# A decay-attention, mixture-of-experts and bilinear kernel: first weights kept unsplit in DRAM, and a new order of the main stage

## The chip, the cores and the metric

The kernel runs on one core of one Trainium2 chip. The metric is device time in microseconds (us) of one execution, from repeated runs; a profile of one more execution shows where that time lies. The engines are TensorE (PE, matrix products; PEld are its weight loads), VectorE (DVE), ScalarE (ACT), GpSimd (POOL) and SyncE (SP, which here only issues transfers).

## The reference

Three parts follow each other, all in 32-bit floats:

```python
# 1. attention with decay: B, H, S, D = 4, 8, 768, 48
f = 1.0 / (1.0 + np.exp(-f_logit))
for t in range(S):
    state = f[:, :, t, :, None] * state + np.einsum('bhd,bhe->bhde', k[:, :, t], v[:, :, t])
    y[:, :, t] = np.einsum('bhd,bhde->bhe', q[:, :, t], state)
x = y.transpose(0, 2, 1, 3).reshape(3072, 384)
# 2. eight experts, weights P from 8 rounds of normalising rows and columns
P = sinkhorn(x @ w_gate)
out = sum(P[:, e:e + 1] * (np.maximum(x @ w1[e], 0.0) @ w2[e]) for e in range(8))   # w1[e]: 384 x 1024
# 3. bilinear
return (out @ w_a) * (out @ w_b) @ w_out                                            # w_a, w_b: 384 x 1536
```

## The kernel before

Every product is made from numbers split in two: a high half `wh`, `xh` rounded to TensorE's fast 32-bit format and a low half `wl`, `xl` that holds the rest. A product costs three matmuls (high by high, high by low, low by high), and ScalarE makes the high half by a copy, VectorE or GpSimd the low half by a subtraction.

An attention stage comes first (to about 421 us); beside it TensorE works on most of expert 0. Everything else is the **main stage**, which this change is about. It has six phases: three of the experts (`moe`, 1024 tokens each) and three of the bilinear part (`out`). A phase is a row of jobs, 19 for `moe`, 8 for `out`, 81 in all. A job has a front and a back.

- `front(n)` (line 975) multiplies a 384 x 384 block of the first weights with the phase's tokens by a fast scheme: 15 products in place of 18 (`CHAINS`), each of three matmuls with 512 columns (`mm`, line 998). For it the block's nine 128 x 128 pieces are turned into 15 sums (`W_SUMS`: 13 additions or subtractions in a buffer `stage` of 15 x 128 columns), and the tokens into 15 sums `xs`. Results stand in banks of PSUM named `pG` and `pF`; ScalarE and VectorE take them into a ring of 19 buffers `z`, handed out by `take_z`/`free_z`.
- `back` (line 1055) splits those results (`halve`: ScalarE, then VectorE or GpSimd) and multiplies them with the second weights in matmuls of 384 columns into `pR` (`gemm_t`, line 368); VectorE adds each `pR` into `acc`.

The first weights of a job are the same in the three phases of its kind. In the first of them (27 jobs: `first_of[kind, u] == n`) `w1_load` (line 814) fetches the pieces into `stage`, `w1_split` (line 844) makes the sums and then, for three groups of 768, 512 and 640 columns (`W_GROUPS`), the halves in `w1t[n % 2]`; `w1_store` (line 865) writes both halves, 1920 KB, to a DRAM buffer `wfd` after chain 9 of the front. In the other 54 jobs `w1_load` fetches both halves back in three transfers and nothing is split. Loads and splits of job n + 2 are put into the list beside the front of job n.

At a phase's start `x_take` (line 902) fetches the 15 sums of the tokens through temporary buffers and splits them; in phases 1, 2, 4 and 5 three of these are cut out of `stage`, which then has no other use. `x_make` (line 879, GpSimd) makes those sums ahead of time, `convert` (line 958) turns 64-bit weights of the bilinear part into 32 bits by seven VectorE steps (lines 311 to 319) during the expert phases, `x2` (line 1117) transposes a phase's result.

The order of every engine's instructions is a list written before the run. `plan.add` records each step with a priority, an engine, a cost and what it reads and writes; `Plan.order` (line 131) plays the steps through and, whenever an engine is free, takes the ready step of least priority. It counts a step as ready some time after its sources end, and a transfer as landed 5 us after it is issued, whatever its size:

```python
    plan = Plan(.4, 1.5, port=True, stay=STAY)   # .4 us from engine to engine, 1.5 us to SP
    LATE = 5.0
...
                far = self.hold if self.ops[u][1] == "SP" else self.slack if ever else self.gap
                gap = late + (far if self.ops[u][1] != eng else 0.0 if eng == "PE" else self.same)
                ready_at[u] = max(ready_at[u], at + cost + gap)
```

Costs marked `"DVE+"` and all of GpSimd's are kept from overlapping in this list. All instructions of line 1203 are those that the main stage's list issues.

## Time and profile before

| | us |
|---|---|
| median of 3 runs (2183.95 to 2189.29) | 2189.18 |
| the profiled execution | 2187.57 |
| its span, first to last instruction | 2185.8 |
| PE busy in the span | 2159.0 |
| DVE, ACT, POOL busy | 1610.4, 942.2, 910.4 |
| moved by transfers | 413.43 MB |

A busy PE is not a PE at its peak, since its matmuls overlap in a pipeline; how fast it goes is read from how long a run of matmuls takes. Idle time of another engine costs nothing by itself.

### The profile page before, as it was taken

The page shows a single profiled execution, that of the slowest core. Times are in us where ns is not written, and L with a number is a line of the kernel's source. Part 1 is how long each engine was busy: PE and PEld are TensorE (multiplying, and loading weights), DVE is VectorE, ACT ScalarE, POOL GpSimd, SP SyncE. Part 2 cuts the span into 40 slices and gives each one's busy share as a digit, 9 for nine tenths or more (in the row PEclk, how much of TensorE's full clock was granted, in tenths as well). Part 3 has the DMA queues.
Part 4 walks back from the last instruction along what each step waited for, and adds up shares of the span by engine and source line. Part 5 has one row for each costly group of instructions (what it writes and reads, how often), then busy time and mean ns, then how long its engine had stood idle before and what let it go on. Part 6 is the DMA issues. An engine that isn't in the chain of part 4 may idle for free.

```text
span 2185.8 us, 41932 instructions
## 1 busy us (share of the span) xinstructions
PE 2159.0 (99%) x15933; PEld 1961.6 (90%) x15933; DVE 1610.4 (74%) x2888; ACT 942.2 (43%) x1779; POOL 910.4 (42%) x924
## 2 busy tenths in 40 slices
PE   8999999999999999999999999999999999999999
PEld 8999999989999999898999988999999888888888
DVE  7878888387878778676787697677776866866755
ACT  3544454454444445433334344433343545533331
POOL 2212121378876664431222255433222577634322
PEclk9999999999999999999999999999999999999999
DMA  6556653456765558875454466666443555787552
GB/s 138 112 118 147 174 122 80 140 201 214 253 245 188 208 187 302 288 250 186 141 173 157 158 225 235 219 218 215 165 163 127 185 203 193 283 284 255 173 173 73
DMA packets 318346, 413.43 MB, mean 189 GB/s; under 512 B 146880, under 2 KB 207936, under 8 KB 314688
## 3 DMA queue, kind: packets, MB, share of 16 engines
q1 hardware_dynamic: 302832, 393.97, 56.0%
q10 hardware_dynamic: 15312, 16.78, 2.2%
q8 instruction: 125, 2.05, 0.4%
q14 instruction: 77, 0.63, 0.1%
HBM read 279.33 MB, written 126.62 MB: 186 GB/s over the span
## 4 chain that ended last, share of the span: by engine, by line
PE 93%; DVE 3%; DMA 2%; SPq 1%; ACT 0%; issue 0%; POOL 0%; ACTq 0%; DVEq 0%
PE pR L368 39%; PE pG L998 27%; PE pF L998 10%; PE pM L356 4%; PE pM L368 3%; PE pT L482 1%; PE pA L525 1%; PE pO L638 1%; PE pA L537 1%; PE pO L610 1%; PE pA L569 1%; PE pO L644 1%; PE pA L580 1%; DVE z L1203 1%; PE pO L682 1%; PE pM L729 0%
## 5 line engine op out<-in xcount | busy, mean ns | idle before, releaser
L368 PE MATMUL pR<-er 128*128 128x384 f32 x5052 | 976.2, 336 | 2.9 <-DVE acc L1203 2.7
L368 PEld LDWEIGHTS pR<-er 128*128 128x128 f32 x5052 | 897.9, 188 | 55.2 <-DVE acc L1203 3.0
L1203 POOL TENSOR_TENSOR er<-z,er 128x512 fp32r<-128x512 f32 x221 | 299.3, 1367 | 659.6 <-ACT er L1203 512.8
L1203 ACT ACTIVATE z<-pG 128x512 f32<-128x512 f32 x474 | 282.8, 599 | 658.6 <-PE pG L998 578.2
L1203 DVE SCALAR_TENSOR_TENSOR acc<-pR,prob,acc 128x384 f32<-128x384 f32 x504 | 305.2, 612 | 194.4 <-PE pR L368 192.8
L998 PE MATMUL pG<-xsh,w 128*128 128x512 f32 x1134 | 431.4, 394 | 5.9 <-ACT z L1203 5.8
L1203 ACT ACTIVATE er<-z 128x512 fp32r<-128x512 f32 x420 | 248.8, 625 | 143.4 <-PE pR L368 107.9
L1203 DVE TENSOR_TENSOR z<-pF,z 128x512 f32<-128x512 f32 x324 | 221.3, 687 | 93.6 <-PE pF L998 70.3
L998 PE MATMUL pG<-er,w 128*128 128x512 f32 x972 | 278.8, 395 | 1.2 <-DVE z L1203 0.8
L998 PEld LDWEIGHTS pG<-xsh,w 128*128 128x128 f32 x1134 | 212.7, 188 | 42.1 <-ACT z L1203 8.1
L1203 DVE TENSOR_TENSOR z<-z,pG 128x512 f32<-128x512 f32 x243 | 166.2, 685 | 84.7 <-PE pG L998 81.2
L998 PE MATMUL pG<-xsl,w 128*128 128x512 f32 x567 | 223.8, 395 | 0.0
L998 PEld LDWEIGHTS pG<-er,w 128*128 128x128 f32 x972 | 180.0, 188 | 32.8 <-DVE z L1203 3.7
L708 POOL TENSOR_TENSOR er<-l,er 128x256 fp32r<-128x256 f32 x84 | 71.7, 854 | 281.0 <-ACT l L706 249.5
L1203 DVE SCALAR_TENSOR_TENSOR er<-z,er 128x512 fp32r<-128x512 f32 x171 | 171.6, 1014 | 6.2 <-ACT er L1203 5.2
L1203 POOL TENSOR_TENSOR stage<-stage 128x128 f32<-128x128 f32 x325 | 158.9, 521 | 38.9 <-DMA stage<-in_moe_w_dram 28.9
L1203 DVE TENSOR_TENSOR z<-pG,z 128x512 f32<-128x512 f32 x174 | 119.9, 689 | 67.3 <-PE pG L998 64.5
L1203 POOL TENSOR_TENSOR w<-stage,w 128x768 fp32r<-128x768 f32 (+2 forms) x75 | 124.1, 1662 | 43.4 <-ACT w L1203 38.8
L998 PE MATMUL pF<-er,w 128*128 128x512 f32 x486 | 139.0, 394 | 1.4 <-DVE z L1203 1.4
L326 POOL TENSOR_TENSOR er<-raw,er 128x384 fp32r<-128x384 f32 (+1 forms) x82 | 94.5, 1157 | 98.5 <-ACT er L324 84.6
L998 PE MATMUL pF<-xsh,w 128*128 128x512 f32 x324 | 126.9, 393 | 0.0
L998 PEld LDWEIGHTS pG<-xsl,w 128*128 128x128 f32 x567 | 106.3, 188 | 10.7
(166 smaller groups left out, 2594.2 us busy)
## 6 DMA issues: line engine op xcount, KB each, us to landing
er<-w2d SPq DMA_DIRECT2D x138, 384.0 KB, 4.5
wfmoe<-w SPq DMA_DIRECT2D x19, 1920.0 KB, 7.8
w<-wfmoe SPq DMA_DIRECT2D x38, 768.0 KB, 5.2
w2d<-er SPq DMA_DIRECT2D x69, 384.0 KB, 4.0
w<-wfmoe SPq DMA_DIRECT2D x38, 640.0 KB, 4.9
w<-wfmoe SPq DMA_DIRECT2D x38, 512.0 KB, 4.3
wfout<-w SPq DMA_DIRECT2D x8, 1920.0 KB, 7.5
raw<-in_moe_w_dram SPq DMA_DIRECT2D x64, 192.0 KB, 2.9
```

The source lines that it names most:

```text
L326: plan.add(prio + 1, "POOL", S_COST[0] + m * S_COST[1], [gk, key], [key], lambda: nc.gpsimd.tensor_tensor(out=lj, in0=got, in1=f32(hj), op ...
L356: nc.tensor.matmul(out=ps, lhsT=a[:, kk, fs], rhs=b[:, kk, :], start=(i == 0), stop=(i == 3 * KD - 1),)
L368: nc.tensor.matmul(out=ps, lhsT=a[:, off:off + 128], rhs=b, start=(start and i == 0), stop=(stop and i == n - 1))
L482: nc.tensor.transpose(ps[0:R, p * 128:p * 128 + 128], src[:, p * 128:p * 128 + R], ident)
L525: nc.tensor.matmul(out=A0[o:o + 64, w, :], lhsT=pct(bk)[r, g, :], rhs=pct(bq)[r, g, :])
L537: nc.tensor.matmul(out=A1[o:o + 56, 0, w, :].rearrange("j (b e) -> j b e", e=8), lhsT=pct(k3)[r, g, 0:56], rhs=qv[r, g, :, 1, :])
L569: nc.tensor.matmul(out=A1[o:o + 48, 1, w, :].rearrange("j (b e) -> j b e", e=16), lhsT=pct(k3)[r, g, 0:48], rhs=qv[r, g, :, 1, :])
L580: nc.tensor.matmul(out=A1[o:o + 32, 0, w, :], lhsT=pct(k3)[r, g, 0:32], rhs=pct(q3)[r, g, 32:64])
L610: nc.tensor.matmul(out=ps[64 * hd:64 * hd + m, p * D:(p + 1) * D], lhsT=kn[64 * c:64 * c + 64, p * R + 64 * hd:p * R + 64 * hd + m], rhs=b ...
L708: op(POOL, .76, [f"hh{ft}", kf], [f"hl{ft}"], lambda hh=hh, hl=hl, hf=hf: nc.gpsimd.tensor_tensor(out=hl, in0=hf, in1=f32(hh), op=ALU.subt ...
L998: nc.tensor.matmul(out=ps, lhsT=a[:, slot], rhs=b, start=(new and i == 0), stop=(i == 2), skip_group_check=not new)
L1203: fn()
```

## The change

Three things, all of the main stage but for the jobs 0 and 1, whose weights are loaded and split in the attention stage.

- **Sums kept unsplit.** `wfd` holds the 15 sums as they stand in `stage` (960 KB a job). They are stored straight after the sums are made; `w1_store` is gone. The other 54 jobs load the three groups into `stage` (384, 256 and 320 KB) and split them as the first jobs do: three copies on ScalarE and three subtractions on GpSimd a job.
- **Temporary buffers.** `stage` is now in use in all phases, so `x_take` has three buffers of the ring `z` in its place at each of the five later phases, taken before the phase's first front.
- **The list.** The main stage is ordered by a new function, `Plan.timed(.03, .3)`. It has tables of how long steps take: `TAKES` by engine and planned cost, and for TensorE `COLUMNS` per matmul with a few ns more at the start of a run (`AFTER`). To another engine go `WAY` and .03 us in place of .4; to SP .3 in place of 1.5. Transfers stand in one queue of 330 GB/s, with 1.93 us of way and .001 us a piece, by sizes from `moves`. VectorE's `"DVE+"` steps and GpSimd's still exclude each other. Priorities and the rule that prefers to stay with one kind of matmul for `STAY` = 1.2 us are the same.

```diff
@@ -97,7 +97,7 @@
     SWITCH = .02
 
     def __init__(self, gap=GAP, hold=GAP, same=SAME, over=0.0, ranked=False, early=0, slack=None, port=False, stay=0.0):
-        self.port, self.shared, self.stay, self.kind = port, set(), stay, {}
+        self.port, self.shared, self.stay, self.kind, self.key = port, set(), stay, {}, {}
         self.ranked, self.early, self.slack = ranked, early, slack or gap
         self.gap, self.hold, self.same, self.over = gap, hold, same, over
         self.ops = []
@@ -106,6 +106,7 @@
     def add(self, prio, eng, cost, reads, writes, fn, late=0.0, fill=False, kind=0):
         n = len(self.ops)
         self.kind[n] = kind
+        self.key[n] = next(iter(writes), ""), len(writes)
         if self.port and eng in ("POOL", "DVE+"):
             self.shared.add(n)
         eng = eng.rstrip("+")
@@ -199,6 +200,106 @@
                     todo.setdefault(self.ops[u][1], []).append(u)
         return made
 
+    ENGINES = ("PE", "DVE", "ACT", "POOL", "SP", "clock")
+    WAY = {"PE": .205, "DVE": .115, "ACT": .125, "POOL": .085}
+    RUNS = {.681: (512, 3), 1.362: (512, 6), .522: (384, 3), 1.044: (384, 6), .53: (384, 3), 1.06: (384, 6),
+            .36: (256, 3), .72: (256, 6), 1.08: (256, 9)}
+    COLUMNS = {512: .2267, 384: .1733, 256: .12}
+    AFTER = {512: (3.7, 6.7, 6.7, -1.2, 4.2, 8.7, 2.5, 5.0, 3.3, 0.0), 384: (-2.5, 3.7, 6.2, 2.5, 3.7, .8, 0.0),
+             256: (2.0,), "pause": (6.0, 6.2, 3.3, 7.5, 3.3, 2.5, 2.5, 2.0, 0.0)}
+    TAKES = {
+        "PE": {.2: .117, .33: .245, .35: .2, .69: .713},
+        "DVE": {.62: .528, .56: .467, .68: .602, .69: .603, .7: .603, .93: .91, 1.0: 1.016, .204: .22, .255: .28, .3: .24, .383: .3},
+        "ACT": {.6: .52, .45: .387, .49: .387, .521: .414, .612: .53, .737: .635, .863: .735, .37: .263, .47: .395, .25: .27},
+        "POOL": {.46: .417, 1.026: .977, 1.252: 1.256, 1.29: 1.256, 1.54: 1.522, 1.828: 1.81, .76: .72},
+        "SP": {.36: .46, .38: .47, .4: .42, .42: .4, .41: .43, .43: .42, .45: .615, 1.2: 1.23, 2.4: 2.5},
+    }
+    DMA_WAY, DMA_RATE, DMA_PIECE = 1.93, 330e3, .001
+
+    def moves(self, n):
+
+        _, eng, cost, _, _, late, _ = self.ops[n]
+        (key, many), cost, kb = self.key[n], round(cost, 3), 1024
+        if eng == "ACT":
+            return (256 * kb, 128) if key[:2] == "xd" else (128 * kb, 128)
+        if cost == .45:
+            return (1920 * kb, 128) if key[:2] == "wf" else (128 * kb * {"0": 6, "1": 4, "2": 5}[key[-1]], 256)
+        if cost == .41:
+            return 64 * kb * many, 128
+        if cost == .43:
+            return 960 * kb, 128
+        if cost == .38:
+            return 384 * kb, 128
+        if key[:2] == "pb":
+            return 256 * kb, 512
+        return (256 * kb if cost == .4 and key[:2] != "sg" else 192 * kb), 128
+
+    def timed(self, near, far, shift={}):
+
+        left, users, ready = [], [[] for _ in self.ops], [0.0] * len(self.ops)
+        todo = {eng: [] for eng in self.ENGINES}
+        prio = [o[0] + shift.get(n, 0) for n, o in enumerate(self.ops)]
+        for n, o in enumerate(self.ops):
+            left.append(len(o[3]))
+            for d in o[3]:
+                users[d].append(n)
+            if not o[3]:
+                todo[o[1]].append(n)
+        free, port, queue, run, now, made = dict.fromkeys(self.ENGINES, 0.0), 0.0, 0.0, 0.0, 0, []
+        width, place, paused = 0, 0, False
+        while any(todo.values()):
+            best = None
+            for eng, ns in todo.items():
+                if ns:
+                    soon = min(ready[n] for n in ns)
+                    at = soon if eng == "clock" else max(free[eng], soon)
+                    if best is None or at < best[0]:
+                        best = (at, eng)
+            at, eng = best
+            n = min((n for n in todo[eng] if ready[n] <= at + 1e-9),
+                    key=lambda n: (eng == "PE" and (self.kind[n] == now) != (run < self.stay), prio[n]))
+            todo[eng].remove(n)
+            cost, late = round(self.ops[n][2], 3), self.ops[n][5]
+            if n in self.shared:
+                at = max(at, port - .03)
+            if eng == "PE" and cost in self.RUNS:
+                cols, count = self.RUNS[cost]
+                if width != cols:
+                    width, place, paused = cols, 0, False
+                if at > free["PE"] + .04:
+                    place, paused = 0, True
+                more = self.AFTER["pause" if paused else cols]
+                takes = 0.0
+                for _ in range(count):
+                    takes += self.COLUMNS[cols] + .001 * more[min(place, len(more) - 1)]
+                    place += 1
+            else:
+                takes = self.TAKES.get(eng, {}).get(cost, cost)
+                if eng == "ACT" and late and cost == .45:
+                    takes = .42
+                if eng == "PE":
+                    width, place, paused = 0, 0, False
+            if n in self.shared:
+                port = max(port, at + takes)
+            if self.kind[n]:
+                run = takes + (run if self.kind[n] == now else 0.0)
+                now = self.kind[n]
+            free[eng] = end = at + takes
+            made.append(self.ops[n][4])
+            dma = eng == "SP" or (eng == "ACT" and late > 0)
+            if dma:
+                size, pieces = self.moves(n)
+                queue = max(end + self.DMA_WAY - .03, queue) + size / self.DMA_RATE + pieces * self.DMA_PIECE
+                end = queue + .03
+            for u in users[n]:
+                to = self.ops[u][1]
+                way = 0.0 if dma or (eng == to and eng != "SP") else self.WAY.get(eng, 0.0) + near
+                ready[u] = max(ready[u], end + way + (far if dma or to == "SP" else 0.0))
+                left[u] -= 1
+                if not left[u]:
+                    todo[to].append(u)
+        return made
+
 
 @with_exitstack
 def tile_decay_attention__then__sinkhorn_moe__then__bilinear_kernel(
@@ -806,7 +907,7 @@
             for u in range(DFF2 // 384):
                 for n in range(2):
                     jobs.append((ph, 2 * u + n, [(n, 384 * u + 128 * f) for f in range(3)], n))
-    wfd = {k: [spill.tile([128, 2, NW, 128], F32, name=f"wf{k}{u}") for u in range(n)] for k, n in (("moe", len(moe_blocks) // 3), ("out", 2 * DFF2 // 384))}
+    wfd = {k: [spill.tile([128, NW, 128], F32, name=f"wf{k}{u}") for u in range(n)] for k, n in (("moe", len(moe_blocks) // 3), ("out", 2 * DFF2 // 384))}
     first_of = {}
     for n, (ph, u, _, _) in enumerate(jobs):
         first_of.setdefault((phases[ph][0], u), n)
@@ -818,8 +919,8 @@
         wh, wl = w1s[n % 2]
         if first_of[kind, u] != n:
             for g, (lo, hi) in enumerate(W_GROUPS):
-                plan.add(prio + W_STEP * g, SP, .45, [f"wf{kind}{u}"], [f"w1{n % 2}{g}"], partial(
-                    nc.sync.dma_start, out=f32(w1t[n % 2][:, :, lo:hi]), in_=wfd[kind][u][:, :, lo:hi]), LATE)
+                plan.add(prio + W_STEP * g, SP, .41, [f"wf{kind}{u}"], [f"sg{x}" for x in range(lo, hi)], partial(
+                    nc.sync.dma_start, out=stage[:, lo:hi], in_=wfd[kind][u][:, lo:hi]), LATE)
             return
         runs = []
         for f, (e, c) in enumerate(blocks):
@@ -845,14 +946,15 @@
 
         ph, u, _, _ = jobs[n]
         kind = phases[ph][0]
-        if first_of[kind, u] != n:
-            return
         wh, wl = w1s[n % 2]
         tt, cs, cl = (nc.gpsimd.tensor_tensor, .46, .00225) if eng == POOL else (nc.vector.tensor_tensor, .26, .0012)
 
-        for i, (o, a, how, b) in enumerate(W_SUMS):
+        for i, (o, a, how, b) in enumerate(W_SUMS if first_of[kind, u] == n else ()):
             plan.add(prio + i, eng, cs, [f"sg{a}", f"sg{b}"], [f"sg{o}"], partial(
                 tt, out=stage[:, o], in0=stage[:, a], in1=stage[:, b], op=getattr(ALU, how)))
+        if first_of[kind, u] == n:
+            plan.add(prio + 15, SP, .43, [f"sg{x}" for x in range(NW)], [f"wf{kind}{u}"], partial(
+                nc.sync.dma_start, out=wfd[kind][u], in_=stage), LATE)
         for g, (lo, hi) in enumerate(W_GROUPS):
             m, at = (hi - lo) * 128, prio + 20 + W_STEP * g
             sg = [f"sg{x}" for x in range(lo, hi)]
@@ -861,14 +963,6 @@
             plan.add(at + 1, eng, .1 + m * cl, sg, [f"w1{n % 2}{g}"], partial(
                 tt, out=wl[:, lo:hi], in0=stage[:, lo:hi], in1=f32(wh[:, lo:hi]),
                 op=ALU.subtract))
-
-    def w1_store(plan, prio, n, after):
-
-        ph, u, _, _ = jobs[n]
-        kind = phases[ph][0]
-        if first_of[kind, u] == n:
-            plan.add(prio, SP, .45, [after] + [f"w1{n % 2}{g}" for g in range(3)], [f"wf{kind}{u}"], partial(
-                nc.sync.dma_start, out=wfd[kind][u], in_=f32(w1t[n % 2])), LATE)
 
     def x_raw(ph, b):
 
@@ -1029,7 +1123,6 @@
                 if i is not None:
                     free_z(kept[i], late)
 
-        w1_store(plan, 1000 * n + SPREAD * 2 // 3, n, f"at{n}-9")
 
     def halve(prio, kind, y, above, eng):
 
@@ -1143,6 +1236,7 @@
 
     y_of = {}
     w2d = {}
+    RAW_USED = (1, 3)
     plan.add(-9000, "clock", 8.0, [], [f"x{(NSTEP - 1) % 4}"], lambda: None)
     expert0(plan, NSTEP // 2 - 2, -8000, "R", p_R[:2], False, 1)
     logits(plan, NSTEP - 1, -4000, "R", p_R[:2])
@@ -1165,7 +1259,10 @@
         base = n - u
         if u == 0:
             if ph:
-                more = l_of + (stage_of if ph != 3 else []) + (raw_of if ph not in (1, 3) else [])
+                extra = [take_z() for _ in range(3)]
+                for z in extra:
+                    free_z(z, 1000 * n + 400)
+                more = l_of + extra + (raw_of if ph not in RAW_USED else [])
                 for i in range(NX):
                     x_take(plan, 1000 * n - 950 + 65 * i, ph, i, POOL if i % 3 != 1 else DVE, more[i % len(more)])
             first = True
@@ -1199,7 +1296,7 @@
             first = False
     assert not later
     with tc.manual_schedule():
-        for fn in plan.order(0.0):
+        for fn in plan.timed(.03, .3):
             fn()
```

## Rows read from the trace of the kernel before

**Rows 1.** Main stage in stretches: length, busy PE, PEld, DVE, ACT, POOL, granted clock, transfers.

```profile
421.40:466.00 44.60, 41.59 (x222) 35.23 (x222) 31.77 (x74) 25.10 (x52) 26.60 (x34) 1.00 0.55 201
466.00:905.00 439.00, 438.81 (x2241) 400.35 (x2241) 347.19 (x523) 203.05 (x361) 309.60 (x356) 1.00 0.67 235
905.00:1356.00 451.00, 443.69 (x2248) 403.06 (x2247) 329.93 (x574) 181.79 (x316) 150.25 (x119) 0.99 0.58 194
1356.00:1801.00 445.00, 442.05 (x2250) 401.99 (x2250) 319.81 (x565) 187.88 (x324) 177.32 (x156) 1.00 0.56 188
1801.00:1935.00 134.00, 131.96 (x646) 116.64 (x647) 99.99 (x144) 64.75 (x116) 80.49 (x92) 1.00 0.70 256
```

**Rows 2.** PE's waits from 421.4 us on: us in total, times, longest.

```profile
PE pG L998 <- ACT z L1203: 5.8, 4, 2.0
PE pR L368 <- DVE acc L1203: 2.7, 1, 2.7
PE pR L1126 <- DVE acc L1203: 2.5, 2, 1.9
PE pF L998 <- DVE z L1203: 1.4, 1, 1.4
PE pR L778 <- DVE prob L769: 1.2, 2, 1.0
```

**Rows 3.** The chain of waits in time around three of them: start, us, what.

```profile
1028.78 7.34 DMA wd<-z
...
1037.35 1.71 PE pG L998 x6
1039.06 3.60 PE pR L368 x12
...
1044.02 2.10 PE pR L368 x12
...
1279.94 1.57 DVE z L315
...
1284.78 1.33 PE pR L368 x3
...
1795.27 9.59 DMA x2d<-z
```

**Rows 4.** Two stretches at the first of these places, columns as in the first group.

```profile
1028.00:1037.00 9.00, 7.48 (x40) 6.64 (x38) 6.10 (x10) 0.79 (x2) 0.47 (x1) 1.00 0.97 335
1039.00:1042.20 3.20, 3.20 (x12) 3.20 (x11) 1.28 (x4) 1.12 (x2) 1.48 (x2) 0.50 0.03 12
```

**Rows 5.** Transfers of the run, count, KB, median us to landing; last, 1020 to 1040 us.

```profile
wfmoe<-w SPq DMA_DIRECT2D x19, 1920.0 KB, 7.8
w<-wfmoe SPq DMA_DIRECT2D x38, 768.0 KB, 5.2
l<-x2d SPq DMA_DIRECT2D x45, 256.0 KB, 4.6
...
w<-wfmoe SPq DMA_DIRECT2D x1, 768.0 KB, 8.7
```

**Rows 6.** Splits of the first weights, instructions by shape: busy us, mean ns, idle before.

```profile
L1203 POOL TENSOR_TENSOR w<-stage,w 128x768 fp32r<-128x768 f32 x25 | 48.9, 1957 | 10.4 <-ACT w L1203 6.1 <-PE pG L998 3.4 <-DVE z L1203 0.8
L1203 POOL TENSOR_TENSOR w<-stage,w 128x640 fp32r<-128x640 f32 x25 | 41.1, 1644 | 12.0 <-ACT w L1203 11.7
L1203 POOL TENSOR_TENSOR w<-stage,w 128x512 fp32r<-128x512 f32 x25 | 34.6, 1386 | 21.0 <-ACT w L1203 21.0
L1203 ACT ACTIVATE w<-stage 128x768 fp32r<-128x768 f32 (+2 forms) x75 | 54.6, 734 | 32.8 <-PE pF L998 10.3 <-PE pG L998 9.8 <-POOL stage L1203 6.1
```

**Rows 7.** VectorE's splits of results: ns min/median/max; then busy us and mean from 466 to 905.

```profile
L1203 DVE SCALAR_TENSOR_TENSOR er<-z,er x171: 673/693/2342, 465.6 to 1777.2; 128x512 fp32r<-128x512 f32 x171
...
L1203 DVE SCALAR_TENSOR_TENSOR er<-z,er 128x512 fp32r<-128x512 f32 x97 | 104.2, 1088 | 1.1 <-ACT er L1203 0.8 <-PE pR L368 0.3
```

**Rows 8.** VectorE's additions of a result, whole run: busy us, mean ns, idle before.

```profile
L1203 DVE SCALAR_TENSOR_TENSOR acc<-pR,prob,acc 128x384 f32<-128x384 f32 x504 | 305.2, 612 | 194.4 <-PE pR L368 192.8
```

## The prediction

> **What bounds the kernel now.** I read the page first, for the busy shares, and then the main stage cut at its phase boundaries [rows 1]. In each row the reader should set PE's busy time against the length of the stretch. From 466 to 905 us, the first expert phase, PE is idle for 439.00 − 438.81 = 0.19 us. The other rows leave 3.01, 7.31, 2.95 and 2.04 us; after 1935 us PE has no gap until the last results are stored. So PE's queue is full, and the whole of what another order or fewer bytes can give back in the main stage is 15.5 us of idle PE, plus what the slow clock costs.
>
> That clock is read next. After PE stood still at 1037 us, the granted clock was 0.50 from 1039.00 to 1042.20 [rows 4], the lower of its two levels (1.2 against 2.4 GHz), and twelve matmuls of 384 columns took 3.60 us against 2.10 us a little later [rows 3]: 1.5 us, and 1.8 us as an estimate with the few matmuls beside them. After the wait at 1284 us three such matmuls took 1.33 us where a quarter of 2.10 is 0.53, so it is at work there too and I count 1.8 us again. The ceiling is 15.5 + 3.6 = 19.1 us, 0.9% of the time.
>
> Then I asked who ended PE's waits [rows 2] and followed the chain of waits back from the three largest [rows 3]. Two kinds show.
>
> *Late transfers.* ScalarE's copy from `pG` into a `z` buffer has to wait for a store that still reads that buffer: 128 KB to `wd` took 7.34 us and 256 KB to `x2d` 9.59 us. In the first case 16 transfer engines were 0.97 busy at 335 GB/s [rows 4], and a 768 KB load of split weights, which has a median of 5.2 us, took 8.7 us beside it [rows 5]. This kind is the 5.8 us under `ACT z` (its four waits taken together; the chain shows the store behind two) and 1.8 us of slow clock: 7.6 us.
>
> *VectorE held up.* At 1279.94 us a step of `convert` took 1.57 us on VectorE, and the `acc` addition that frees `pR` stood behind it in the queue. This kind is 2.7 + 2.5 + 1.4 us and 1.8 us of clock: 8.4 us. The rest, 19.1 − 7.6 − 8.4 = 3.1 us, is mostly the start of the expert weights' normalisation (1.2 us under `prob`) and is kept.
>
> **The change, part by part.** *Bytes.* 54 jobs load 960 KB in place of 1920, and 27 store 960 in place of 1920: 81 × 960 KB = 80 MB of 413 MB. PE waits for none of these transfers directly [rows 2]; what they can give is that a short store is no longer queued behind them, that is the first kind. I take three quarters of it: −5.7 us (bounds 0 and −7.6).
>
> *GpSimd and ScalarE.* Each of the 54 jobs gets three subtractions on GpSimd, 1.957 + 1.644 + 1.386 = 4.99 us [rows 6], 269 us in all, and three copies on ScalarE, 3 × 0.734 = 2.2 us, 119 us in all. From 905 to 1356 us (19 jobs) GpSimd goes from 150 to 150 + 95 = 245 us of 451, or 54%, and ScalarE from 182 to 224 us, 50%. The first phase had GpSimd at 309.60 of 439, 71%, and VectorE at 79%, with PE idle for 0.19 us [rows 1]. This is the cover, and I cost the work itself at nothing: it has been there in a heavier form. If the cover were gone, each job would lose up to the 1.96 us of the longest subtraction, 54 × 1.96 = 106 us at the very most.
>
> VectorE feels it all the same. Its split `er<-z,er` takes 0.673 to 2.342 us, median 0.693 over the run, and 1.088 us on average in the first phase [rows 7]: with two operands in SBUF it is held up while GpSimd works. The Trainium skill, "SBUF — State Buffer", section "Who interferes with whom", states that GpSimd and a VectorE instruction with two SBUF inputs take one port pair and that the second to come blocks until the first is done. The trace agrees: 2.342 − 0.673 = 1.67 us is about one subtraction of 640 columns. By this rule alone the change would cost time; by the rows of the first phase it costs none until it pushes back an addition that PE needs. That case is a rival below.
>
> *The second kind.* The new list knows how long VectorE's steps take and still keeps `convert` and GpSimd apart, but there is more of GpSimd's work to keep apart. I take half of the 8.4 us as gone: −4.2 us (bounds −8.4 and +8.4, its doubling, as GpSimd's work near it grows by 95/150 or more).
>
> *Margins of the list.* Its allowance from engine to engine falls from 0.4 to about 0.15 us (way plus 0.03), and steps are costed at what they take: an `acc` addition 0.528 + 0.115 = 0.643 us to its reader against 0.612 us measured [rows 8]. A store of 1920 KB by its formula takes 1.93 + 1966/330 + 0.13 = 8.0 us against 7.8, a 768 KB load 1.93 + 786/330 + 0.26 = 4.6 against 5.2 [rows 5]. So prices fit the trace, and PE's list can place a step sooner; but a source that comes 0.1 us late now stops PE, where before it had room. Nothing in the trace measures this. From below it is nothing (a stopped PE lets the others catch up); from above I set 0.3 us in each of 81 jobs, 24 us, as if half the 0.6 us of one addition came out wrong once a job. I take 0.02 us a job, +1.6 us, near the lower end because plain steps hardly vary (median 0.693 against a minimum of 0.673).
>
> *Borrowed buffers.* Five phase starts lend three `z` buffers to `x_take`, each for a load of 4.6 us [rows 5], a copy of some 0.7 and a subtraction of 1.4 us, 6.7 us a time. `stage` lent them before at four of the starts, at no cost to the fronts; `z` is what the fronts write. From below nothing (16 more buffers); from above the longest wait seen where such a buffer was late, 2.0 us [rows 2], five times, 10 us. I take +0.8 us.
>
> *The attention stage.* Two stores of 960 KB move there from the main stage, onto SP ahead of the next transfers of the attention rows. They take about 5 us, as the 768 KB load does; PE has expert 0 to fill the time. From below nothing, from above 5 us each, 10 us; I take +0.5 us.
>
> SP's queue otherwise has the same count of loads and stores; the store now waits for the sums instead of for chain 9, so it stands earlier, and behind it the next raw load of `stage`, which had to wait for the later splits anyway. Taken as nothing.
>
> The sum is −5.7 − 4.2 + 1.6 + 0.8 + 0.5 = −7.0 us. Against the profiled execution, 2187.57 us, that is **2180.6 us**, −0.32%. The profiled execution lies 1.6 us under the median of the three runs (2189.18) and 3.6 over the lowest (2183.95). About 0.3%, 6.6 us, is what a measurement of this kernel can tell from no change, so the forecast stands at the edge of it: faster lies below 2181.0, slower above 2194.1.
>
> **The rivals.**
> - *All of it comes back* (chance 0.22). The list foresees every wait: 2187.6 − 16.0 (both kinds) + 0.5 = 2172.1 us, as low as 2168.5 with the full 19.1. For: the first phase shows 439 us with 0.19 us idle under a worse list. Against: the borders of phases, where everything comes at once.
> - *The forecast*, 2174 to 2184 us (0.37).
> - *Waits move* (0.22). The old waits go, −9.9, but `x_take`'s hold on `z` costs 2 us at each of five starts: 2187.6 − 9.9 + 10 + 0.5 = 2188.2 us. For: the largest kind of wait now is of a copy that finds its `z` still in use. Against: the transfers that hold them become shorter.
> - *Slower by thin margins* (0.13). PE meets a late source in every job; with the gain of 9.9 us and the 0.5 us of attention it is slower by over 0.3% from (6.6 + 9.4)/81 = 0.20 us a job on; at 0.3 us it gives 2187.6 − 9.4 + 24.3 = 2202.5 us. Against: a steady full queue, in which one late step gives all later ones room.
> - *Slower by the port* (0.06). One in ten of the 162 new subtractions holds up a VectorE split by 1.67 us with a needed addition behind it: 16 × 1.67 = 27 us, 2187.6 − 9.4 + 27 = 2205 us; it decides from 10 such cases on. This is the mechanism that the Trainium skill, "SBUF — State Buffer", section "Who interferes with whom", states. Against it stands the first phase, with more GpSimd work and no wait.
>
> That the list doesn't do what it says (its prices are wrong) is the first slower rival; the fits above speak against it.
>
> **How the numbers follow.** Faster takes the first rival (0.22), the larger part of the forecast's own range (7.0 of 10 us, 0.27) and a little of "waits move" (0.02): 0.51. Slower takes the last two (0.19) and 0.02 of "waits move": 0.21. The rest is 0.28. The range that leaves out no more than 2 in 10 goes from 2169, next to the ceiling, to 2196, which takes in the "waits move" case and the beginnings of the slower ones; the forecast's own is 2174 to 2184.
>
> **What would show it.** In the profile of the changed kernel: PE idle from 421 us to the last front below 10 us, and no or one stretch at clock 0.50; about 335 MB moved; GpSimd near 1180 us busy, ScalarE near 1060; median landing of `wd<-z` and `x2d<-z` shorter, and no PE wait that goes back to them. Wrong would be: PE waits of 0.1 to 0.4 us by the dozen (thin margins); PE's waits at the phase borders under `ACT z` with `x_take`'s subtraction behind (borrowed buffers); VectorE's `er<-z,er` at 1.1 us in all phases with `acc` waits on PE (port); an attention stage longer than 421 us.

## The result and the profile after

The changed kernel takes 2202.6 us (median of 6 runs, 2200.77 to 2207.24) against 2188.93 us before; the ratio is 1.0063, with a 95% interval of 1.0049 to 1.0077. It is slower by 13.7 us, and outside the range given. The profiled execution took 2200.77 us with a span of 2199.0 us, 13.2 us more than before.

The main stage in stretches, columns as in [rows 1], and one of the stretches at slow clock:

```profile
421.40:466.00 44.60, 40.31 (x218) 34.60 (x217) 31.61 (x73) 22.40 (x47) 22.79 (x31) 1.00 0.36 122
466.00:905.00 439.00, 435.22 (x2211) 395.73 (x2210) 352.84 (x516) 209.73 (x369) 330.73 (x368) 1.00 0.56 188
905.00:1356.00 451.00, 446.31 (x2274) 406.14 (x2273) 358.88 (x580) 218.32 (x375) 231.18 (x161) 1.00 0.46 149
1356.00:1801.00 445.00, 437.15 (x2202) 395.59 (x2201) 332.20 (x550) 210.87 (x363) 252.96 (x210) 0.99 0.45 148
1801.00:1935.00 134.00, 132.06 (x645) 114.99 (x644) 107.82 (x146) 72.49 (x129) 104.32 (x109) 1.00 0.56 187
...
1322.30:1325.70 3.40, 3.40 (x10) 2.84 (x9) 2.69 (x5) 0.85 (x2) 0.61 (x1) 0.50 0.57 154
```

PE's idle time in these five stretches is 4.29 + 3.78 + 4.69 + 7.85 + 1.94 = 22.55 us, where [rows 1] had 15.5. Three more stretches like the last row, with the clock at 0.50, lie at 878.6, 1359.9 and 1735.3 us: four in all, in order of time after waits of PE for VectorE of 2.0, 2.9, 1.9 and 2.6 us, where there were two. At 1.8 us each that is another 3.6 us. So 10.7 of the 13.2 us are idle time of PE in these stretches and slow clock. Of the rest, 1.0 us is idle time of PE before and after them, and about 1.5 us is longer busy time that these rows do not explain. The attention stage is as long as before (the first front starts at 421.3 us, before at 421.4).

Bytes and load are as forecast: 333.84 MB moved, GpSimd 1181.0 us busy, ScalarE 1044.3. VectorE has the same 2888 instructions and is busy for 1681.2 us in place of 1610.4. That is the first trace of the cause: 41.1 of these 70.8 us are the 420 steps of `convert`, which take 196.7 us before and 237.8 after (sums over their lines).

PE's waits from 421.4 us on, to be set beside [rows 2] (L1300 is now the line of all that the list issues, L1092 that of the front's matmuls, L469 that of the back's):

```profile
PE pG L1092 <- DVE z L1300: 8.9, 12, 2.0
PE pR L469 <- DVE acc L1300: 6.7, 4, 2.9
PE pG L1092 <- ACT z L1300: 3.6, 5, 1.4
PE pR L879 <- DVE prob L870: 2.8, 2, 2.2
```

The wait for ScalarE has fallen from 5.8 to 3.6 us, and none of ScalarE's own waits ends with a store of `wd` or `x2d` any more (a store of `x2d` now lands after 2.5 us, median, before after 5.7). The waits for VectorE's `z` and `acc` went from 7.4 us [rows 2, with 0.8 us of `pG` not shown there] to 15.6. The chain of waits before the longest of them, start and us:

```profile
1314.99 1.11 DVE z L416
...
1316.12 1.41 DVE z L418
...
1317.55 1.26 DVE z L419
...
1318.84 1.37 DVE z L420
1320.20 0.54 DVE acc L1300
...
1320.78 2.01 PE pR L469 x9
```

Lines 412 to 420 are the steps of `convert` (311 to 319 before). To read what they wait for, the timeline of the same place, first VectorE, then GpSimd, and of another place for comparison (start, us, line, operation, out and in):

```profile
1314.91 1.17 DVE L416 SCALAR_TENSOR_TENSOR z<-z,z 128x256 f32<-128x256 uint32 x1
1316.12 1.40 DVE L418 TENSOR_TENSOR z<-z 128x256 f32<-128x256 f32 x1
1317.55 1.25 DVE L419 TENSOR_SCALAR z<-z 128x256 int32<-128x256 int32 x1
...
1314.21 1.60 POOL L1300 TENSOR_TENSOR w<-stage,w 128x640 fp32r<-128x640 f32 x1
1315.77 2.89 POOL L1300 TENSOR_TENSOR er<-z,er 128x512 fp32r<-128x512 f32 x2
1318.61 2.73 POOL L1300 TENSOR_TENSOR l<-l,l 128x512 f32<-128x512 f32 x2
...
865.63 0.29 DVE L415 TENSOR_SCALAR z<-z 128x256 int32<-128x256 int32 x1
...
866.42 0.42 DVE L418 TENSOR_TENSOR z<-z 128x256 f32<-128x256 f32 x1
...
863.97 1.34 POOL L1300 TENSOR_TENSOR er<-z,er 128x512 fp32r<-128x512 f32 x1
866.54 1.45 POOL L1300 TENSOR_TENSOR er<-l,er 128x512 fp32r<-128x512 f32 x1 [1.23 <-PE pG L1092]
```

At the first place each GpSimd step starts as the one before it ends, and the VectorE steps end one by one as GpSimd steps do: L418 starts at 1316.12, after a GpSimd step has begun at 1315.77, and takes 1.40 us. The same instruction at 866.42 starts in a gap of GpSimd (its step from 863.97 ended at 865.31, and the next begins only at 866.54) and takes 0.42 us. So at the first place VectorE gets one short step through per GpSimd step. Behind the fourth of them stands the `acc` addition that PE waits for until 1320.78, and then the clock falls.

### The profile page after: what moved, and what is told of

Read it like the earlier page. It is cut to its first block, busy times and chain, and to the rows that moved or that the text cites. A ratio compares the mean times of both kernels' runs of the same rounds, so it can differ in the third digit from the quotient of the medians.

```text
span 2199.0 us, 42449 instructions
## 1 busy us (share of the span) xinstructions
PE 2164.2 (98%) x15933; PEld 1961.2 (89%) x15933; DVE 1681.2 (76%) x2888; ACT 1044.3 (47%) x1941; POOL 1181.0 (54%) x1086
## 2 busy tenths in 40 slices
DMA packets 297614, 333.84 MB, mean 152 GB/s; under 512 B 146880, under 2 KB 207936, under 8 KB 297408
## 4 chain that ended last, share of the span: by engine, by line
PE 90%; DVE 6%; issue 1%; ACT 1%; DMA 1%; SPq 1%; POOL 0%; ACTq 0%; DVEq 0%; POOLq 0%
PE pR L469 37%; PE pG L1092 27%; PE pF L1092 9%; PE pM L457 4%; PE pM L469 4%; DVE z L1300 1%; PE pT L583 1%; DVE er L1300 1%; PE pA L626 1%; PE pO L739 1%; PE pA L638 1%; PE pO L745 1%; PE pA L670 1%; PE pO L711 1%; PE pA L681 1%
## 5 line engine op out<-in xcount | busy, mean ns | idle before, releaser
L469 PE MATMUL pR<-er 128*128 128x384 f32 x5052 | 978.1, 336 | 6.7 <-DVE acc L1300 6.7
L469 PEld LDWEIGHTS pR<-er 128*128 128x128 f32 x5052 | 897.4, 188 | 61.0 <-DVE acc L1300 8.3
L1300 POOL TENSOR_TENSOR w<-stage,w 128x768 fp32r<-128x768 f32 (+2 forms) x237 | 392.2, 1658 | 326.2 <-ACT w L1300 274.9
L1300 ACT ACTIVATE z<-pG 128x512 f32<-128x512 f32 x474 | 282.1, 597 | 467.4 <-PE pG L1092 408.1
L1300 POOL TENSOR_TENSOR er<-z,er 128x512 fp32r<-128x512 f32 x231 | 314.2, 1372 | 254.9 <-ACT er L1300 186.0
L1092 PE MATMUL pG<-xsh,w 128*128 128x512 f32 x1134 | 434.0, 397 | 8.2 <-DVE z L1300 4.4
L1300 DVE SCALAR_TENSOR_TENSOR acc<-pR,prob,acc 128x384 f32<-128x384 f32 x504 | 303.7, 611 | 159.4 <-PE pR L469 158.4
L1300 ACT ACTIVATE er<-z 128x512 fp32r<-128x512 f32 x435 | 256.5, 624 | 138.7 <-PE pR L469 64.8
L1092 PE MATMUL pG<-er,w 128*128 128x512 f32 x972 | 279.7, 396 | 4.8 <-DVE z L1300 4.5
L1300 DVE TENSOR_TENSOR z<-pF,z 128x512 f32<-128x512 f32 x324 | 221.2, 686 | 71.2 <-PE pF L1092 50.2
L1092 PEld LDWEIGHTS pG<-xsh,w 128*128 128x128 f32 x1134 | 214.0, 189 | 51.0 <-ACT z L1300 8.1
L1300 ACT ACTIVATE w<-stage 128x768 fp32r<-128x768 f32 (+2 forms) x237 | 173.9, 736 | 172.8 <-PE pF L1092 65.7
L1092 PE MATMUL pG<-xsl,w 128*128 128x512 f32 x567 | 224.7, 396 | 0.0
L1300 DVE TENSOR_TENSOR z<-z,pG 128x512 f32<-128x512 f32 x243 | 166.0, 683 | 70.9 <-PE pG L1092 68.3
L1092 PEld LDWEIGHTS pG<-er,w 128*128 128x128 f32 x972 | 179.3, 188 | 33.8 <-DVE z L1300 8.1
L1300 DVE SCALAR_TENSOR_TENSOR er<-z,er 128x512 fp32r<-128x512 f32 x171 | 180.2, 1059 | 17.7 <-ACT er L1300 15.7
L1300 POOL TENSOR_TENSOR stage<-stage 128x128 f32<-128x128 f32 x325 | 162.8, 518 | 29.7 <-DMA stage<-in_moe_w_dram 13.5
L1300 DVE TENSOR_TENSOR z<-pG,z 128x512 f32<-128x512 f32 x174 | 119.5, 687 | 54.8 <-PE pG L1092 52.3
L1092 PE MATMUL pF<-er,w 128*128 128x512 f32 x486 | 139.5, 395 | 0.0
L1092 PE MATMUL pF<-xsh,w 128*128 128x512 f32 x324 | 126.9, 393 | 0.0
```

Of the source, the lines that this page charges most:

```text
L469: nc.tensor.matmul(out=ps, lhsT=a[:, off:off + 128], rhs=b, start=(start and i == 0), stop=(stop and i == n - 1))
L1092: nc.tensor.matmul(out=ps, lhsT=a[:, slot], rhs=b, start=(new and i == 0), stop=(i == 2), skip_group_check=not new)
L1300: fn()
```

## The experiments

"Before" was run beside each on the same chip (medians 2188.4 to 2189.5 us). Theories: **P**, the added GpSimd subtractions hold up VectorE at the port; **L**, the new list's thin margins; **Z**, the borrowed `z` buffers. P was later sharpened to **R** and **B**, as the expectations say.

**Halves of the change.** The old list over the new work, and the new list over the old work:

```diff
-        for fn in plan.timed(.03, .3):
+        for fn in plan.order(0.0):
```

> The changed kernel with the list of before (its margins of 0.4 and 1.5 us, 5 us a transfer) over the new work: sums stored unsplit, splits in every phase, borrowed z buffers. If the added subtractions on GpSimd hold up VectorE (theory P), it is about as slow as the changed kernel or slower, 2200 to 2215 us. If the new list with its thin margins is the cause (theory L), it comes back to the time of before, 2182 to 2192 us.

Measured: 2195.52 us, ratio 1.0035 (1.0021 to 1.005). For the other half, `timed` and its tables were put into the kernel before:

> The kernel before with the new list alone: both halves stored and fetched, no splits in the later phases, no borrowed buffers. Theory P: no loss is left, 2172 to 2190 us, with fewer waits of PE than before. Theory L: the whole loss is here, 2198 to 2206 us.

Measured: 2184.36 us, ratio 0.9976 (0.9964 to 0.9988). The list alone gains 4.8 us, and the new storage with its splits and borrowed buffers costs 6.4 under the old list; together they cost 13.7, some 12 more than their sum. The first time lies between the ranges of P and L, the second in P's; neither theory foretold both.

**Margins.** `timed(.2, 1.2)`, and as a null change `timed(.05, .35)`; the latter also for the new list alone:

> The changed kernel with wider margins in the new list (0.2 us in place of 0.03 between engines, 1.2 in place of 0.3 to SyncE). Theory L: waits go, 2185 to 2195 us. Theory P: the margin is not what is missing, within 4 us of 2202.6 us.

> The changed kernel with margins of 0.05 and 0.35 us in place of 0.03 and 0.3 in the new list: a change that no theory gives a meaning, to see how far the time moves when the list only falls out another way. If the loss has a steady cause: 2199 to 2206 us. If it is an accident of one list: anything from 2185 to 2210 us.

> The kernel before with the new list alone, with margins of 0.05 and 0.35 us in place of 0.03 and 0.3: the same slight change that moved the changed kernel by 10 us. Theory R: without the added GpSimd work few steps meet at the port and an exact list holds, 2181 to 2189 us. If the new list is brittle in itself: it moves by 5 us or more from 2184.4 us.

Measured: 2205.74 us (1.0065 to 1.0099), 2212.43 us (1.0091 to 1.0122) and 2187.06 us (0.998 to 0.9999). Wider margins do not help, so L falls as it stood. But a change of 0.02 us in a margin moves the changed kernel by 10 us and the new list alone by 3: with the splits in it, much depends on how a list happens to fall. A difference of a few us between two lists, each made anew, can therefore not be put down to the edit that separates them.

**Borrowed buffers.** Once without borrowing in the changed kernel (`more = l_of + own + ...`, `own` one buffer), once with it in the new list alone:

> The changed kernel in which x_take borrows no z buffer: in place of three it has one buffer of its own (what SBUF still holds) beside l and raw. Theory Z (borrowed z buffers at the phase starts are the cause): most of the loss goes, 2185 to 2194 us, and the waits of PE near the phase starts shrink. Other theories: within 4 us of 2202.6 us, or slower since x_take has fewer buffers.

> The kernel before with the new list and with x_take borrowing three z buffers in place of the three cut from stage; weights stored and fetched in both halves. Theory Z: the loss is here, 2196 to 2205 us. If the splits anew are the cause, it stays with the new list alone, 2181 to 2188 us.

Measured: 2201.19 us (1.0041 to 1.0071) and 2185.96 us (0.9977 to 0.9996). Z falls: both times lie far from its ranges. They moved by 1.4 us to the faster and 1.6 us to the slower side, less than a list made anew moves by itself. With these two, the new function has ordered the new work in four lists, 2201.2 to 2212.4 us, and the old work in three, 2184.4 to 2187.1 us; so the 12 us by which the halves cost more together rest on more than one list.

**The subtractions.** First left out of the plan, so that the list is made anew; then left out of the changed kernel's own order, which the other instructions keep exactly; then in that order with the first 128 columns alone; and as a control ScalarE's copies of the same splits left out of it (in the edits, the lines above the dots are the first of these, those below the second):

```diff
+            if first_of[kind, u] != n:
+                continue
             plan.add(at + 1, eng, .1 + m * cl, sg, [f"w1{n % 2}{g}"], partial(
...
-                op=ALU.subtract))
+                op=ALU.subtract) if first_of[kind, u] == n else lambda: None)
```

> The changed kernel without the subtraction that makes the weights' low half in the 54 later jobs (their low halves stay those of an earlier job); loads, ScalarE's copies, list and borrowed buffers stay. GpSimd has 269 us less to do. Theory P: the loss is gone, 2172 to 2190 us, and steps of convert take their bare 0.2 to 0.4 us again. Theory L, or borrowed buffers as the cause: no gain, 2198 to 2206 us.

> The changed kernel in exactly its own order on every engine, but the 162 subtractions of the later phases are not issued (low halves stay those of an earlier job). Unlike the run that left them out of the plan too, nothing else moves. Theory P (they hold up VectorE): 2180 to 2192 us. If they matter only through the list that is made around them: within 3 us of 2202.6 us.

> The changed kernel in exactly its own order on every engine, with each of the 162 subtractions cut to its first 128 columns (the other columns of the low half stay those of an earlier job): the same instructions and waits, but 0.46 us of GpSimd in place of 1.3 to 1.9. Theory R: near the run without them, 2187 to 2194 us. If the mere presence of the instructions and their waits costs the time: 2199 to 2205 us.

> The changed kernel in its own order, with ScalarE's 162 copies of the later phases not issued (high halves stay those of an earlier job); the GpSimd subtractions stay. Theory R: ScalarE has no part in it, 2197 to 2205 us. If any work left out of a fixed order gives the time back: 2186 to 2194 us.

Measured: 2203.74 us (1.0049 to 1.0096) anew; in the same order 2189.06 us (0.9989 to 1.0008) without, 2190.19 us (0.9993 to 1.0013) with short ones, 2203.89 us (1.0054 to 1.0084) without the copies. The three runs in the same order lie in the ranges of P and R; the one made anew does not. PE's waits in the same order, first without the subtractions (the profiled execution, 2193.63 us, was the slowest of ten), then without the copies:

```profile
PE pR L469 <- DVE acc L1300: 4.1, 2, 2.6
PE pG L1092 <- DVE z L1300: 3.6, 6, 1.5
```
```profile
PE pR L469 <- DVE acc L1300: 7.9, 5, 2.9
PE pG L1092 <- DVE z L1300: 6.4, 11, 1.5
```

Busy time, first of the changed kernel, then of the same order without the subtractions:

```profile
PE 2164.2 (98%) x15933; PEld 1961.2 (89%) x15933; DVE 1681.2 (76%) x2888; ACT 1044.3 (47%) x1941; POOL 1181.0 (54%) x1086
```
```profile
PE 2166.1 (99%) x15933; PEld 1967.1 (90%) x15933; DVE 1621.4 (74%) x2888; ACT 1045.5 (48%) x1941; POOL 914.5 (42%) x924
```

The same 2888 VectorE instructions in the same order take 59.8 us less when GpSimd's subtractions are gone; the `convert` steps among them take 205.5 us in place of 237.8, with short subtractions 209.3, without the copies 244.9. So, in this order, it is the time for which the subtractions occupy GpSimd, not their presence, their waits, or just any work taken out, and it acts by making VectorE's steps longer. In a list made anew it does not hold; that is taken up below.

**The other side of the collision.** The changed kernel's own order, all subtractions in, `convert`'s 420 steps on VectorE not issued (the bilinear weights are then not converted):

```diff
-                     ... [rk], [ck], fn)
+                     ... [rk], [ck], lambda: None)
```

> The changed kernel in its own order on every engine, with the 420 conversion steps on VectorE not issued (the bilinear weights are then whatever stands in the buffers). All added GpSimd subtractions stay. Theory R (VectorE's short steps come to the port behind long GpSimd steps, each waits for a whole one, and the additions that PE needs stand behind them): most of the loss goes, 2184 to 2192 us. If the subtractions cost time in another way: 2198 to 2205 us.

Measured: 2180.82 us, ratio 0.9966 (0.9953 to 0.9978). In stretches, the two phases that hold 52 of the 60 conversions:

```profile
905.00:1356.00 451.00, 451.00 (x2312) 411.47 (x2311) 269.69 (x400) 223.59 (x385) 234.28 (x165) 1.00 0.47 154
1356.00:1801.00 445.00, 445.00 (x2264) 404.71 (x2263) 266.35 (x404) 216.54 (x372) 262.79 (x228) 1.00 0.44 148
```

PE does not stand still for a moment in 896 us, with GpSimd at 234 and 263 us, as busy as in the changed kernel. Its waits for `acc` fell to 0.8 us. The time lies below R's range: 21.8 us are gained where 13.7 were lost. Leaving the conversions out takes away long waits that the kernel before had too, and over 200 us of VectorE's work besides. So the run shows that the subtractions cost PE next to nothing where no conversion meets them; it doesn't by itself separate a meeting at the port from VectorE's load, since no other VectorE work was left out as a control. The longer steps of the runs before it speak for the meeting.

**Ways out.** Smaller pieces (256 columns), the subtractions on VectorE, a list that counts `x_take`'s GpSimd steps (they are entered as `"POOL+"`, which `add` does not take for a step that uses the port, so that not all of GpSimd's steps are kept apart from VectorE's as the description of the kernel has it), conversions kept away from the phase starts, both, and both without the new splits:

```diff
-        if self.port and eng in ("POOL", "DVE+"):
+        if self.port and eng in ("POOL", "POOL+", "DVE+"):
...
-    CONVERTS = {(0, u): 1 for u in range(3, 19, 2)} | {(p, u): 1 + (u % 3 == 2 or u == 9) for p in (1, 2) for u in range(19)}
+    CONVERTS = {(0, u): 1 for u in range(1, 16, 2)} | {(p, u): 2 - (u in (3, 9)) for p in (1, 2) for u in range(2, 16)}
```

> The changed kernel with the 162 subtractions of the later phases cut into pieces of at most 256 columns (405 instructions of 0.46 to 0.76 us in place of 162 of 1.3 to 1.9). Theory R: what costs time is that VectorE's two-operand steps come to the shared port a little late, find one long GpSimd step in front and wait for all of it; shorter steps make each such wait shorter, 2190 to 2199 us though GpSimd has more to do. If GpSimd's total work is what counts, it is no faster than the changed kernel, 2200 to 2212 us.

> The changed kernel with those 162 subtractions on VectorE (about 0.7 to 1 us each) in place of GpSimd. Theory R: VectorE gets 54 x 2.5 = 135 us more work but is held up less, 2187 to 2198 us. If VectorE's load is what counts, it is slower than the changed kernel, 2203 to 2215 us.

> The changed kernel whose list counts x_take's GpSimd subtractions among the steps that exclude VectorE's two-operand ones. Theory B (the list is blind to them, and VectorE's steps land on top of them at the phase starts): 2187 to 2197 us, with fewer long conversion steps where PE waits. If blindness isn't it: 2199 to 2210 us.

> The changed kernel with the 60 conversions kept out of the first two and last three jobs of a phase; the list stays blind to x_take's GpSimd work. Theory B: what meets at the phase starts is conversion and x_take, so most of the loss goes, 2186 to 2196 us. Otherwise 2199 to 2208 us.

> Both: the list counts x_take's GpSimd work, and conversions stay off the phase starts. Theory B: the best with the new splits, 2183 to 2192 us. Otherwise 2199 to 2208 us.

> The kernel before (both halves stored and fetched) with the new list, the list counting x_take's GpSimd work, and conversions off the phase starts. Theory B: better than the new list alone (2184.4 us), 2175 to 2182 us. Otherwise no better than that, 2184 to 2190 us.

Measured, in this order: 2201.74 us (1.0039 to 1.0069), 2200.44 us (1.0036 to 1.0066), 2198.08 us (1.0028 to 1.0059), 2199.76 us (1.0033 to 1.007), 2196.45 us (1.0025 to 1.0053), 2196.76 us (1.0023 to 1.0052). None came into the range of R or B. The smaller pieces (432 instructions in the trace, not 405) fall where GpSimd's total work is said to count, and the moved conversions (in the first phase they now begin in its second job) where B is said to be wrong; the others lie in no range. Gains of 3 to 6 us under B are less than a slight change of a margin moves this kernel by, so B is not shown. The last is the plainest miss: the new list alone lost 12.4 us by the two edits together. With two conversions in most jobs, PE waits for VectorE's `z`, first there and then in the new list alone:

```profile
PE pG L1099 <- DVE z L1304: 11.6, 11, 2.8
```
```profile
PE pG L1099 <- DVE z L1304: 4.0, 6, 1.0
```

The longest of these waits ends at 918.3 us, behind three conversion steps of 1.31 to 1.38 us that meet three of GpSimd's splits of results (3.98 us from 912.63 on). Yet the 420 conversion steps take 203.4 us in this run and 202.1 in the new list alone: they are not held up more in all, only elsewhere. The fastest kernel that does the whole work is the new list alone, 2184.36 us.

## Why the prediction was wrong, step by step

- **Ceiling and bound** (PE full, 19.1 us to win): right; most of the loss is idle PE and slow clock too. No run came near the ceiling: the one without conversions still has 8.2 us of idle PE between 421.4 and 1935 us.
- **Bytes, −5.7 us**: the size fits, the reason is not shown. The wait for ScalarE fell by 2.2 us and its slow clock (1.8 us) is gone: 4.0 us. But PE's wait for ScalarE's `z` falls still further by either half of the change, first with the old list and the new bytes, then with the new list and the bytes of before, and in the latter no slow clock is left in the main stage either:

```profile
PE pG L1092 <- ACT z L1300: 1.0, 2, 0.7
```
```profile
PE pG L1099 <- ACT z L1304: 1.2, 5, 0.4
```

- **GpSimd and ScalarE at nothing**: for GpSimd it failed here; for ScalarE it held, since without its copies nothing is gained (2203.89 us). The amounts were right (270.6 us more on GpSimd against 269; 102.1 on ScalarE against 119), the cover was not. I took the first phase, 71% GpSimd with 0.19 us of idle PE, as proof that the work can be borne. Steps were held up there too (the splits took 1.088 us on average [rows 7]), but with so little idle PE none of them kept PE waiting for long. That phase has 8 of the 60 conversions; the two after it have 26 each, 182 short VectorE steps a phase. Once the conversions are gone, these two phases bear the same GpSimd work with no idle PE. So the share of time is no measure; what counts is which steps meet and what stands behind them.
- **The second kind, −4.2 us**: wrong sign, and the largest error. PE's waits for VectorE went from 7.4 to 15.6 us, and all four slow clocks now follow one of them, where one did: with 1.8 us for each, 9.2 us became 22.8, +13.6 in place of −4.2 and beyond the upper bound of +8.4. I took GpSimd's growth beside it too lightly. Nor does the new list halve these waits where GpSimd has no more to do: in the new list alone they are 6.9 us. The chain of the kernel before had shown how it comes about: behind the conversion step of 1.57 us [rows 3] stand two more long ones and the `acc` addition that PE waits for:

```profile
1281.54 1.40 DVE z L317
...
1282.96 1.24 DVE z L318
1284.20 0.54 DVE acc L1203
```

- **Margins, +1.6 us**: no steady price per job was seen; wider ones didn't help. Yet the list is part of it: the two halves of the change cost 12 us more together than apart.
- **Borrowed buffers, +0.8 us**: not told from nothing. **Attention, +0.5 us**: not told from nothing either; 0.6 us more of idle PE before 421.4 us.
- **The rival that came true** is "slower by the port", to which I gave 0.06 with 2205 us; measured were 2202.6. That the number is so near is partly luck: it counted on a gain of 9.4 us, of which 4.0 came, and on held-up splits, where mostly conversion steps were held up (VectorE's splits into `er`, five more of them, grew from 199.0 to 215.5 us, the conversions by 41.1). "Slower by thin margins" stood at 2202.5 us, and what it said did not come true. For the port rival the Trainium skill, "SBUF — State Buffer", section "Who interferes with whom", was cited. The timeline agrees with it: an L418 step, which has two inputs in SBUF and takes 0.42 us, takes 1.40 us when a GpSimd step has begun before it.

What stays open: lists made anew without the subtractions, with small ones, or with them on VectorE are as slow as the changed kernel (2200.4 to 2203.7 us), although in its own order they account for all of the loss. So the subtractions are the cause in this one order, and not the only way to lose the time. In the list without them the `convert` steps take 209.9 us, hardly more than in the new list alone, but four of them meet GpSimd's older steps just where PE waits next, first VectorE, then GpSimd:

```profile
1276.20 1.46 DVE L414 SCALAR_TENSOR_TENSOR z<-z,z 128x256 int32<-128x256 int32 x1
1277.69 1.27 DVE L415 TENSOR_SCALAR z<-z 128x256 int32<-128x256 int32 x1
1278.99 1.40 DVE L416 SCALAR_TENSOR_TENSOR z<-z,z 128x256 f32<-128x256 uint32 x1
1280.43 1.38 DVE L418 TENSOR_TENSOR z<-z 128x256 f32<-128x256 f32 x1
...
1276.08 1.30 POOL L1302 TENSOR_TENSOR xsl<-l,xsh 128x512 fp32r<-128x512 f32 x1 [6.68 <-ACT xsh L1302]
1277.34 4.18 POOL L1302 TENSOR_TENSOR er<-z,er 128x512 fp32r<-128x512 f32 x3
```

Another 5.1 us of its waits for VectorE's `z` fall between 1801 and 1935 us, where no conversion is left. With the subtractions on VectorE the largest wait is for ScalarE's `z`, 7.5 us. These lists share ScalarE's copies and the loads through `stage`, and no run makes a list anew without those. I did not find what makes one list put a meeting where PE waits more often than another; an order made for longer GpSimd steps may leave room that a list made to fit does not, but that is argued, not shown.

## What to carry to other kernels

Work put on an engine that is half idle is not free if its steps hold up those of a busy one: before counting on the idle share, look in the trace for the short steps of the other engine that would meet it, what stands behind them in their queue, and whether the stretch taken as proof has as many of them. To tell a work's own cost from that of a list made anew around it, leave it out of a fixed order, with another piece of work left out as a control. Run the parts of a change apart as well as together: here one part alone gained 4.8 us and the whole lost 13.7. And when a list is made anew for every edit, make a slight change without meaning too, to see how far the time moves by itself; here it was 10 us.

## What the runs showed of the hardware

Between GpSimd steps that follow without a gap, VectorE got one waiting step through for each, so four conversion steps of 0.3 to 0.4 us took 1.17 to 1.40 us each at 1315 us. GpSimd's own steps of that kind, with a median of 1.30 us over the run, took 1.45 there (two in 2.89 at 1315.77). A step with one input tensor is held up as well: the `TENSOR_SCALAR` of L419 took 1.25 us at 1317.55, and its median over the run is 0.29.
